# Second mixing of talking-heads attention: the last 64 keys of two neighbouring tiles in one matmul, with the values held in five blocks

## The chip, the cores and the metric

The kernel runs on one core of a Trainium2 chip. The metric is device time in microseconds (us). The kernel before takes 595.45 us as the median of three runs (595.12 to 597.32). The engines in the profile are PE (TensorE, matmuls), PEld (its weight loads), DVE (VectorE), ACT (ScalarE), POOL (GpSimd) and SP (which issues DMAs).

## The reference

Attention with two mixings over heads, followed by a feed-forward layer with squared ReLU. There are 8 batches, 12 heads, 448 positions and a head size of 64; the layer goes from 768 to 2048 to 768 features.

```python
scores = scale * np.matmul(q, k.transpose(0, 1, 3, 2))
scores = np.einsum('bhij,hg->bgij', scores, w_pre)       # first mixing
scores = scores - np.max(scores, axis=-1, keepdims=True)
attn = np.exp(scores)
attn = attn / (np.sum(attn, axis=-1, keepdims=True) + 1e-09)
attn = np.einsum('bhij,hg->bgij', attn, w_post)          # second mixing
out = np.matmul(attn, v)
h = np.maximum(x @ w_in, 0.0)      # x: out with the heads side by side
return h * h @ w_out
```

## The kernel before

The work goes in 360 steps, 45 for each batch. A step handles one tile of 10 queries (`IQ`; the last tile of a batch has 8) with all 12 heads, which is 120 rows (`RG`) of 448 keys.

Scores of 128 queries at a time are made by `score_burst` and copied out of PSUM by ACT and VectorE. DMAs on the SP queue (`gather`) then put the rows of one tile, query by query with its heads, into one buffer `G`. For the first 20 tiles of batch 0 (`FUSED`) there is no gather; the queries are multiplied by the mixing weights on VectorE instead (`mix_queries`).

`mix` (L391) is the first half of a step. One matmul with a 120x120 matrix mixes the heads (L402); ACT takes the exponential `e` and its row sums `sm` (L405); VectorE takes the reciprocals `rc` (L407); POOL multiplies the rows of the second mixing's matrix `post` by them, giving `pn` (L409). So the division by the row sum is done on the small matrix and not on `e`.

`unmix` (L413) is the second half, four steps later (`LAG`). Four matmuls (L422) take 128 keys of `e` each as the stationary side and `pn` as the moving side, 120 columns. They turn the tile around (keys on partitions) and mix the heads. 448 keys are three blocks of 128 and one of 64. The fourth matmul takes keys 320 to 447, so that its lower 64 partitions repeat keys of the third block. All four land in one PSUM bank, and VectorE casts the 480 columns to `at` (L424).

After 15 tiles, a third of a batch, two `av_unit`s (L212) multiply by the values, six heads each. Per head there are four matmuls of 150 columns, one for each block of keys (L220). Two heads run beside each other, one in each half of the array's columns and of PSUM's partitions. ACT copies the result to `xt`. The values lie in `vts`, four blocks; the fourth has real rows in its upper 64 partitions alone, and zeros in the lower ones, set once by a memset (L165). `load_v` brings the values by POOL-issued DMAs, some 29 steps or more ahead of a batch's first value product for batches 2 to 7.

`ffn1_unit` (L260, with the ReLU on ACT and the squaring on POOL or VectorE, L271) and `ffn2_unit` (L304) are the feed-forward layer.

The order of TensorE's and POOL's instructions is the order in which the program writes them (`manual_schedule`). Feed-forward work of the batch before is put between `mix` and `unmix` in portions (`fill`), by fixed weights for each unit. VectorE's, ACT's and SP's order is made by the language's planner, which takes the dependencies and an estimate of each instruction's time. All PSUM tiles share one pool of eight banks.

Of the kernel before, what the change touches and what calls it, by code (L numbers as in the profile page):

```python
# [8 lines left out]
BF16 = mybir.dt.bfloat16  # L9
F32 = mybir.dt.float32  # L10
ACT = mybir.ActivationFunctionType
ALU = mybir.AluOpType
PE, POOL = mybir.EngineType.PE, mybir.EngineType.Pool

B, H, S, D = 8, 12, 448, 64
# [4 lines left out]
R = 4  # L20
RQ = 7
PQ = S // RQ
HQ = H // 2
IQ = 10
NT = 45
RG = H * IQ
FUSED = 20
# [10 lines left out]
TT = 15  # L38
TQ = TT * IQ
# [14 lines left out]
def kernel(  # L54
# [11 lines left out]
    nc = tc.nc  # L66
    P = nc.NUM_PARTITIONS

    consts = ctx.enter_context(tc.tile_pool(name="consts", bufs=1))
    wts = ctx.enter_context(tc.tile_pool(name="wts", bufs=1))  # L70
    stage = ctx.enter_context(tc.tile_pool(name="stage", bufs=1))
    work = ctx.enter_context(tc.tile_pool(name="work", bufs=1))
    atp = ctx.enter_context(tc.tile_pool(name="atp", bufs=1))
# [3 lines left out]
    def bank(name, dtype=F32):  # L77
        return psp.tile([P, 512 if dtype == F32 else 1024], dtype, name=name, tag="ps")
# [21 lines left out]
    def wcol(w, name, eng):  # L100
# [7 lines left out]
                      in_=bass.AP(tensor=w_pre.tensor, offset=w_pre[0, 0:1].offset, ap=[[0, P], [1, H * H]]))  # L108
# [24 lines left out]
    for t in range(3 * P // IQ, NT):  # L133
        n0, n = max(0, 3 * P - IQ * t), min(IQ, S - IQ * t)
# [11 lines left out]
    post = consts.tile([P, H, IQ], BF16, name="post")  # L146
    nc.vector.tensor_tensor(out=post[0:RG, :, :], in0=istripe[0:RG, :].unsqueeze(1).to_broadcast([RG, H, IQ]),
                            in1=col_post[0:RG, :].unsqueeze(2).to_broadcast([RG, H, IQ]), op=ALU.mult)
    post = post[:, :, :].rearrange("p g i -> p (g i)")
# [7 lines left out]
    post_gi = consts.tile([P, H, IQ], BF16, name="post_gi")  # L157
    nc.vector.tensor_tensor(out=post_gi[0:RG, :, :], in0=stripe_gi[0:RG, :].unsqueeze(1).to_broadcast([RG, H, IQ]),
                            in1=col_gi[0:RG, :].unsqueeze(2).to_broadcast([RG, H, IQ]), op=ALU.mult)
    post_gi = post_gi[:, :, :].rearrange("p g i -> p (g i)")  # L160
    ND = LAG + 2
    ets = [consts.tile([P, S], BF16, name=f"e{x}") for x in range(ND)]
    vts = [stage.tile([P, H, R, D], BF16, name=f"v{x}") for x in range(2)]
    for t in vts:
        nc.vector.memset(t[0:PQ, :, R - 1, :], 0.0)  # L165

    attn = [atp.tile([P, R, H, TQ], BF16, name=f"at{x}") for x in range(2)]
    w1 = [wts.tile([P, NPAIR, DFF // 2], BF16, name=f"w1_{x}") for x in range(2)]
    w2 = [wts.tile([P, FT // 4, DMODEL], BF16, name=f"w2_{x}") for x in range(4)]

    qTs, kTs, xts, h2ts, ats = {}, {}, {}, {}, {}
# [40 lines left out]
    def av_unit(b, third, cp):  # L212

        at = ats[(b, third)]
        ps = bank("ot_ps")
        for y in range(3):
            for r in range(R):
                for hh in range(2):
                    g = 6 * cp + 2 * y + hh
                    nc.tensor.matmul(ps[64 * hh:64 * hh + 64, TQ * y:TQ * y + TQ], lhsT=vts[b % 2][:, g, r, :],  # L220
                                     rhs=at[:, r, g, :], start=(y == 0 and r == 0), stop=(r == R - 1),
                                     skip_group_check=True)
        if b not in xts:
            xts[b] = ffnp.tile([P, NPAIR, S], BF16, name="xt", tag="xt", bufs=2)
        n = min(TQ, S - TQ * third)
        nc.scalar.copy(out=xts[b][:, 3 * cp:3 * cp + 3, TQ * third:TQ * third + n],  # L226
                       in_=ps[:, 0:3 * TQ].rearrange("p (y t) -> p y t", t=TQ)[:, :, 0:n])

    def av_units(b, third):
        return [(800, lambda cp=cp: av_unit(b, third, cp)) for cp in range(2)]  # L230
# [96 lines left out]
    Sb, Gs, esb = {}, {}, {}  # L327
# [27 lines left out]
    def rows_of(t):  # L355
        return H * min(IQ, S - IQ * t)
# [23 lines left out]
    def fused_part(t, u):  # L380

        if t not in parts:
            parts[t] = [0, bank("m_ps")]
        if parts[t][0] > u:
            return
        parts[t][0] = u + 1
        for y in range(2):
            nc.tensor.matmul(parts[t][1][0:RG, 0:S], rhs=kTs[0][:, u + 3 * y, :], lhsT=mixed(u, y, t, t + 1),  # L388
                             start=(u + y == 0), stop=(u + 3 * y == NPAIR - 1))

    def mix(s):  # L391
        n = rows_of(s[1])
        b, t = s
        fused = b == 0 and t < FUSED
        if fused:
            for u in range(NPAIR // 2):
                fused_part(t, u)
            ps = parts[t][1]
        else:
            ps = bank("m_ps")  # L400
            m = pres[max(x for x in pres if x <= t)] if b else pre
            nc.tensor.matmul(ps[0:n, 0:S], lhsT=m[0:n, 0:n], rhs=Gs.pop(s)[0:n, :], start=True, stop=True)  # L402
        e = ets[(NT * s[0] + s[1]) % ND]
        sm = work.tile([P, 1], F32, name="sm", tag="sm", bufs=4)
        nc.scalar.activation(out=e[0:n, 0:S], in_=ps[0:n, 0:S], func=ACT.Exp, scale=SCALE, accum_out=sm[0:n, 0:1])  # L405
        rc = work.tile([P, 1], F32, name="rc", tag="rc", bufs=4)
        nc.vector.reciprocal(out=rc[0:n, :], in_=sm[0:n, :])  # L407
        pn = work.tile([P, RG], BF16, name="pn", tag="pn", bufs=LAG + 2)
        nc.gpsimd.tensor_scalar(out=pn[0:n, :], in0=(post_gi if fused else post)[0:n, :], scalar1=rc[0:n, 0:1], scalar2=1.0,  # L409
                                op0=ALU.mult, op1=ALU.mult)  # L410
        esb[s] = (e, pn)

    def unmix(s):  # L413
        b, t = s
        n = rows_of(t)
        third, tl = divmod(t, TT)
        if (b, third) not in ats:
            ats[(b, third)] = attn[(3 * b + third) % 2]
        e, pn = esb.pop(s)
        ps = bank("at_ps")  # L420
        for r in range(R):
            nc.tensor.matmul(ps[:, RG * r:RG * r + RG], lhsT=e[0:n, min(P * r, S - P):min(P * r, S - P) + P], rhs=pn[0:n, :],  # L422
                             start=True, stop=True)
        nc.vector.tensor_copy(out=ats[(b, third)][:, :, :, IQ * tl:IQ * tl + IQ],  # L424
                              in_=ps[:, 0:R * RG].rearrange("p (r g i) -> p r g i", r=R, i=IQ))

    filler = []
    owed = [0.0]
# [17 lines left out]
    with tc.manual_schedule(engines={PE, POOL}):  # L446
# [39 lines left out]
        for i in range(-1, end):  # L486
# [9 lines left out]
            if s0:  # L496
                b, t = s0
# [9 lines left out]
            if s0:  # L507
                mix(s0)
# [4 lines left out]
            if s1:  # L513
                unmix(s1)
                b1, t1 = s1
                if t1 % TT == TT - 1:
                    for u in av_units(b1, t1 // TT):
                        at_step(i + 3, u)
                if t1 == NT - 1:
                    at_step(i + 3 if b1 else FFN2_AT, (0, lambda b1=b1: filler.extend(ffn_units(b1))))  # L520
# [4 lines left out]
            for _ in range(2 if i >= GATHERS_AT else 0):  # L525
# [8 lines left out]
                if nxt < len(blocks) and t2 - FIRST[b2][blk2] in first:  # L534
                    x = first.index(t2 - FIRST[b2][blk2])
# [37 lines left out]
```

## Time and profile before

| | |
|---|---|
| median of three runs | 595.45 us |
| profiled execution | 597.58 us, span 595.5 us |
| TensorE busy, share of the span | 573.0 us, 96% |
| VectorE busy | 411.7 us, 69% |
| ScalarE busy | 381.5 us, 64% |
| GpSimd busy | 311.7 us, 52% |
| granted TensorE clock, mean | 0.997 |
| L422, second mixing | 1440 matmuls, 134.9 us busy |
| L424, cast of its result | 360, mean 650 ns |
| L220, value product | 1152 matmuls, 42.2 us busy |
| L407, reciprocal | 360, mean 159 ns |
| L409, `pn` | 360, mean 370 ns |

Matmuls overlap, so that the mean duration of one (216 ns at L422) is longer than its share of TensorE's time. What one is worth is read from the chain of waits, which gives the path its times. Busy shares are means over the span; the windows by stage show the first batches apart from the rest.

### The profile page before, as it was taken

How to read it: one execution, taken by the hardware profiler on the slowest of the kernel's cores; microseconds unless marked ns; L12 is line 12 of the kernel's file. 1: busy time of each engine (PE TensorE's matmuls, PEld its weight loads, DVE VectorE, ACT ScalarE, POOL GpSimd, SP SyncE). 2: the span in 40 equal slices, each digit the busy share in tenths (PEclk: the TensorE clock that was granted, in tenths of full speed). 3: DMA queues.
4: the chain of work that ended last, by engine and by line, in shares of the span. 5: the costliest groups of instructions: out<-in, count | busy, mean ns of one | idle time of the engine just before them, and what ended most of it. 6: DMA issues, size and time to landing. Idle time of an engine off the chain costs nothing.

```text
span 595.5 us, 18405 instructions
## 1 busy us (share of the span) xinstructions
PE 573.0 (96%) x6615; PEld 370.2 (62%) x6615; DVE 411.7 (69%) x1073; ACT 381.5 (64%) x1114; POOL 311.7 (52%) x692
## 2 busy tenths in 40 slices
PE   3998999999999999999999999999999999999997
PEld 2576777666566665666665665666665665666554
DVE  7657669888767777767877678777867767666011
ACT  3645888677876557865776548775777648762410
POOL 6344885343677227762577326772386325761740
PEclk9998999999999999999999999999999999999999
DMA  9898899689568754696557855786544855432113
GB/s 130 136 181 156 144 206 184 141 141 196 118 117 135 160 117 89 113 149 140 107 96 129 157 119 100 117 136 141 121 74 65 138 120 105 86 49 54 28 26 81
DMA packets 79307, 71.49 MB, mean 120 GB/s; under 512 B 12496, under 2 KB 74224, under 8 KB 79216
## 3 DMA queue, kind: packets, MB, share of 16 engines
q1 hardware_dynamic: 49354, 47.30, 36.6%
q0 software_dynamic: 29280, 22.81, 28.3%
q8 instruction: 52, 0.85, 0.6%
q10 hardware_dynamic: 582, 0.21, 0.2%
q14 instruction: 39, 0.32, 0.1%
HBM read 45.70 MB, written 11.01 MB: 95 GB/s over the span
## 4 chain that ended last, share of the span: by engine, by line
PE 86%; DMA 4%; ACT 4%; issue 2%; POOL 1%; DVE 1%; SPq 0%; ACTq 0%; DVEq 0%; POOLq 0%
PE o_ps L304 24%; PE h_ps L260 24%; PE at_ps L422 12%; PE m_ps L402 10%; PE ot_ps L220 6%; PE m_ps L388 4%; PE s_ps L341 4%; DMA G<-S 3%; ACT e L405 2%; PE tr_ps L205 2%; ACT S L351 1%; DMA kst<-in_k_dram 1%; PE s_ps L347 1%; ACT hr L266 1%; POOL qst L87 1%
## 5 line engine op out<-in xcount | busy, mean ns | idle before, releaser
L424 DVE CAST at<-at_ps 128x480 bf16<-128x480 f32 x360 | 228.5, 650 | 67.4 <-PE at_ps L422 66.7
L405 ACT ACTIVATE e<-m_ps 120x448 bf16<-120x448 f32 x360 | 196.1, 550 | 90.2 <-PE m_ps L402 77.8
L409 POOL TENSOR_SCALAR pn<-post,rc 120x120 bf16<-120x120 bf16 (+1 forms) x340 | 125.3, 370 | 212.8 <-DVE rc L407 123.5
L260 PE MATMUL h_ps<-xt,w 128*128 128x448 bf16 (+2 forms) x960 | 169.7, 316 | 1.2 <-ACT e L405 0.7
L304 PE MATMUL o_ps<-w,h 128*128 128x384 bf16 x768 | 138.7, 326 | 0.0
L422 PE MATMUL at_ps<-pn,e 120*128 120x120 bf16 (+1 forms) x1440 | 134.9, 216 | 1.1 <-ACT S L351 1.0
L422 PEld LDWEIGHTS <-e 120*128 120x128 bf16 (+1 forms) x1440 | 104.7, 98 | 44.0 <-ACT S L351 2.2
L402 PE MATMUL m_ps<-G,pre 120*120 120x448 bf16 (+1 forms) x340 | 121.9, 358 | 1.6 <-ACT S L351 0.7
L260 PEld LDWEIGHTS <-w 128*128 128x128 bf16 x960 | 85.2, 98 | 58.0 <-issue 6.9
L271 POOL TENSOR_TENSOR h<-hr 128x384 bf16<-128x384 f32 (+1 forms) x144 | 106.1, 739 | 22.2 <-ACT hr L266 19.0
L266 ACT ACTIVATE hr<-h_ps 128x448 f32<-128x448 f32 (+2 forms) x160 | 75.5, 478 | 49.5 <-PE h_ps L260 32.8
L304 PEld LDWEIGHTS <-h 128*128 128x128 bf16 x768 | 73.0, 98 | 45.5 <-issue 2.5
L407 DVE RECIPROCAL rc<-sm 120x1 f32<-120x1 f32 x360 | 57.1, 159 | 49.5 <-ACT e L405 41.0
L351 ACT CAST S<-s_ps 128x448 bf16<-128x448 f32 x177 | 82.3, 548 | 13.2 <-PE s_ps L341 10.8
L353 DVE CAST S<-s_ps 128x448 bf16<-128x448 f32 x141 | 79.5, 615 | 2.7 <-DMA G<-S 1.4
L405 ACT ACTIVATION_READ_ACCUMULATOR e<-m_ps 120x1 f32 x360 | 75.2, 209 | 0.0
L313 DVE COPY osb<-o_ps 128x384 f32<-128x384 f32 x54 | 30.0, 556 | 49.4 <-PE o_ps L304 49.0
L402 PEld LDWEIGHTS <-pre 120*120 120x120 bf16 (+1 forms) x340 | 45.0, 132 | 21.7 <-issue 12.7
L220 PE MATMUL ot_ps<-at,v 128*64 128x150 bf16 x1152 | 42.2, 229 | 0.1
L226 ACT CAST xt<-ot_ps 128x450 bf16<-128x450 f32 (+1 forms) x48 | 25.5, 533 | 26.3 <-PE ot_ps L220 25.7
L341 PE MATMUL s_ps<-kT,qT 64*128 64x448 bf16 x276 | 40.9, 360 | 0.9 <-ACT e L405 0.5
L220 PEld LDWEIGHTS <-v 128*64 128x64 bf16 x1152 | 38.0, 109 | 4.0 <-issue 3.4
(51 smaller groups left out, 281.5 us busy)
## 6 DMA issues: line engine op xcount, KB each, us to landing
G<-S SPq DMA_DIRECT2D x276, 105.0 KB
out_dram<-osb SPq DMA_DIRECT2D x54, 192.0 KB
kst<-in_k_dram POOLq DMA_DIRECT2D x14, 336.0 KB, 6.6
qst<-in_q_dram POOLq DMA_DIRECT2D x14, 336.0 KB, 6.7
G<-S SPq DMA_DIRECT2D x70, 52.5 KB
v<-in_v_dram POOLq DMA_DIRECT2D x8, 384.0 KB, 9.7
w<-in_moe_w_in_dram POOLq DMA_DIRECT2D x6, 512.0 KB, 9.6
w<-in_moe_w_out_dram POOLq DMA_DIRECT2D x8, 384.0 KB, 8.1
```

What stands on the lines that cost most here:

```text
L220: nc.tensor.matmul(ps[64 * hh:64 * hh + 64, TQ * y:TQ * y + TQ], lhsT=vts[b % 2][:, g, r, :], rhs=at[:, r, g, :], start=(y == 0 and r == 0 ...
L260: nc.tensor.matmul(ps[:, 0:n], lhsT=w1[ft // 8][:, c2, ft % 8 * 128:ft % 8 * 128 + 128], rhs=xts[b][:, c2, n0:n1], start=(c2 == 0), stop=( ...
L266: nc.scalar.activation(out=hr[:, 0:n], in_=ps[:, 0:n], func=ACT.Relu)
L271: eng.tensor_tensor(out=dst[:, x - o:y - o], in0=hr[:, x - n0:y - n0], in1=hr[:, x - n0:y - n0], op=ALU.mult)
L304: nc.tensor.matmul(ps[:, 0:384], lhsT=lhsT, rhs=w2[ft // 4][:, ft % 4, nt * 384:(nt + 1) * 384], start=(ft == 0), stop=(ft == FT - 1))
L351: nc.scalar.copy(out=sb[:, h, :], in_=ps[:, 0:S])
L353: nc.vector.tensor_copy(out=sb[:, h, :], in_=ps[:, 0:S])
L402: nc.tensor.matmul(ps[0:n, 0:S], lhsT=m[0:n, 0:n], rhs=Gs.pop(s)[0:n, :], start=True, stop=True)
L405: nc.scalar.activation(out=e[0:n, 0:S], in_=ps[0:n, 0:S], func=ACT.Exp, scale=SCALE, accum_out=sm[0:n, 0:1])
L409: nc.gpsimd.tensor_scalar(out=pn[0:n, :], in0=(post_gi if fused else post)[0:n, :], scalar1=rc[0:n, 0:1], scalar2=1.0, op0=ALU.mult, op1=A ...
L422: nc.tensor.matmul(ps[:, RG * r:RG * r + RG], lhsT=e[0:n, min(P * r, S - P):min(P * r, S - P) + P], rhs=pn[0:n, :], start=True, stop=True)
L424: nc.vector.tensor_copy(out=ats[(b, third)][:, :, :, IQ * tl:IQ * tl + IQ], in_=ps[:, 0:R * RG].rearrange("p (r g i) -> p r g i", r=R, i=IQ))
```

## The change

In each third, tile 0 stands alone and the tiles 1 and 2, 3 and 4, up to 13 and 14 are pairs. `mix` now also divides the last 64 keys' exponentials of its tile by the row sum and writes them into one half of a buffer `en` that the two tiles of a pair share: lower half for an even tile, upper half for an odd one. This runs on VectorE, for the first 30 tiles of batch 0 on POOL. `unmix` keeps its first three matmuls. The fourth is done for even tiles alone: `en`, both halves, is the stationary side, and the undivided matrix `post` the moving one. It gives the last 64 keys of the even tile on the lower partitions and those of the odd tile before it on the upper ones. For odd tiles the cast takes 360 columns instead of 480.

In the value product the first three blocks stay as they were. The fourth becomes two matmuls, one for the eight even tiles (80 columns) and one for the seven odd ones (70 columns, which lie in the places of the even tiles behind them). Both go over every second group of ten columns. The even ones need the last 64 keys' values on the lower partitions: a fifth block of `vts`, whose lower half is a copy of the fourth block's upper half, made on VectorE once a batch, and whose upper half is zero.

```diff
     ets = [consts.tile([P, S], BF16, name=f"e{x}") for x in range(ND)]
-    vts = [stage.tile([P, H, R, D], BF16, name=f"v{x}") for x in range(2)]
+    ens = [consts.tile([P, 2, PQ], BF16, name=f"en{x}") for x in range(ND)]
+    for t in ens:
+        nc.vector.memset(t[:, :, :], 0.0)
+    vts = [stage.tile([P, H, R + 1, D], BF16, name=f"v{x}") for x in range(2)]
     for t in vts:
         nc.vector.memset(t[0:PQ, :, R - 1, :], 0.0)
-
-    attn = [atp.tile([P, R, H, TQ], BF16, name=f"at{x}") for x in range(2)]
+        nc.vector.memset(t[PQ:P, :, R, :], 0.0)
+
+    attn = [atp.tile([P, R, H, TT, IQ], BF16, name=f"at{x}") for x in range(2)]
...
     def av_unit(b, third, cp):
         at = ats[(b, third)]
+        if cp == 0 and third == 0:
+            nc.vector.tensor_copy(out=vts[b % 2][0:PQ, :, R, :], in_=vts[b % 2][PQ:P, :, R - 1, :])
         ps = bank("ot_ps")
         for y in range(3):
-            for r in range(R):
+            for r in range(R - 1):
                 for hh in range(2):
                     g = 6 * cp + 2 * y + hh
                     nc.tensor.matmul(ps[64 * hh:64 * hh + 64, TQ * y:TQ * y + TQ], lhsT=vts[b % 2][:, g, r, :],
-                                     rhs=at[:, r, g, :], start=(y == 0 and r == 0), stop=(r == R - 1),
+                                     rhs=at[:, r, g, :, :].rearrange("p t i -> p (t i)"),
+                                     start=(y == 0 and r == 0), stop=False, skip_group_check=True)
+            for x in range(2):
+                for hh in range(2):
+                    g = 6 * cp + 2 * y + hh
+                    cols = ps[64 * hh:64 * hh + 64, TQ * y:TQ * y + TQ].rearrange("p (t i) -> p t i", i=IQ)
+                    nc.tensor.matmul(cols[:, x:TT:2, :], lhsT=vts[b % 2][:, g, R - x, :],
+                                     rhs=at[:, R - 1, g, 2 * x:TT:2, :], start=False, stop=True,
                                      skip_group_check=True)
...
-        esb[s] = (e, pn)
+        en = ens[(8 * (3 * b + t // TT) + (t % TT + 1) // 2) % ND]
+        eng = nc.gpsimd if b == 0 and t < 2 * TT else nc.vector
+        eng.tensor_scalar(out=en[0:n, t % TT % 2, :], in0=e[0:n, S - PQ:S], scalar1=rc[0:n, 0:1], scalar2=1.0,
+                          op0=ALU.mult, op1=ALU.mult)
+        esb[s] = (e, pn, en)
...
-        e, pn = esb.pop(s)
+        e, pn, en = esb.pop(s)
         ps = bank("at_ps")
-        for r in range(R):
-            nc.tensor.matmul(ps[:, RG * r:RG * r + RG], lhsT=e[0:n, min(P * r, S - P):min(P * r, S - P) + P], rhs=pn[0:n, :],
+        for r in range(R - 1):
+            nc.tensor.matmul(ps[:, RG * r:RG * r + RG], lhsT=e[0:n, P * r:P * r + P], rhs=pn[0:n, :], start=True, stop=True)
+        k = R - 1 if tl % 2 else R
+        if k == R:
+            mat = post_gi if b == 0 and t < FUSED else post
+            nc.tensor.matmul(ps[:, RG * (R - 1):RG * R], lhsT=en[0:RG, :, :].rearrange("p x k -> p (x k)"), rhs=mat[0:RG, :],
                              start=True, stop=True)
-        nc.vector.tensor_copy(out=ats[(b, third)][:, :, :, IQ * tl:IQ * tl + IQ],
-                              in_=ps[:, 0:R * RG].rearrange("p (r g i) -> p r g i", r=R, i=IQ))
+        nc.vector.tensor_copy(out=ats[(b, third)][:, 0:k, :, tl, :],
+                              in_=ps[:, 0:k * RG].rearrange("p (r g i) -> p r g i", r=k, i=IQ))
```

## The prediction

> **What bounds the kernel now.** I read the page's busy shares and the clock row first, then who waited for whom, then the chain of waits, because the chain says what one instruction of each kind is worth on the path.
>
> ```profile
> PE 573.0 (96%) x6615; PEld 370.2 (62%) x6615; DVE 411.7 (69%) x1073; ACT 381.5 (64%) x1114; POOL 311.7 (52%) x692
> ...
> PE 86%; DMA 4%; ACT 4%; issue 2%; POOL 1%; DVE 1%; SPq 0%; ACTq 0%; DVEq 0%; POOLq 0%
> ```
>
> TensorE is busy 96% of the span and is 86% of the chain that ended last. Stage by stage (time, then busy time of each engine):
>
> ```profile
> 0.00:20.00 20.00, 9.69 (x188) 5.57 (x188) 14.12 (x38) 7.42 (x15) 10.92 (x23) 1.00 0.92 134
> 20.00:90.00 70.00, 66.88 (x887) 49.90 (x887) 48.07 (x132) 50.59 (x166) 43.13 (x98) 0.98 0.93 166
> 90.00:150.00 60.00, 57.26 (x868) 40.09 (x868) 51.79 (x161) 45.00 (x145) 25.96 (x60) 1.00 0.88 164
> 150.00:550.00 400.00, 398.14 (x4406) 251.20 (x4405) 293.07 (x736) 268.04 (x772) 214.42 (x481) 1.00 0.62 113
> ```
>
> From 150 to 550 us TensorE is idle 1.9 us of 400: whatever leaves its queue there comes off the time. From 20 to 150 us it is idle 5.9 us, so part of a saving may turn into waiting. VectorE is the second engine: 73% busy from 150 to 550 us, but 86% from 90 to 150 us. The chain of waits, a stretch of it (start, length, instructions):
>
> ```profile
> 281.56 0.21 PE at_ps L422 x4
> 281.77 0.19 PE m_ps L402
> 281.96 1.30 PE o_ps L304 x8
> ...
> 283.67 0.86 PE tr_ps L205 x84
> 284.52 1.69 PE ot_ps L220 x48
> ```
>
> One matmul of the second mixing (120 columns) is 0.21/4 = 52.5 ns of path. A 384-column one is 1.30/8 = 162.5 ns, one of 448 is 190 ns; the difference, 27.5 ns for 64 columns, is 0.43 ns a column, and 120 x 0.43 = 52 shows that weight loads are hidden. The value product is two matmuls side by side in half the array: 1.69/24 = 70.4 ns a pair, 64.5 of it streaming 150 columns and 5.9 over.
>
> **Part by part.**
>
> Removed: the fourth matmul of seven tiles in each third of 15. 8 batches x 3 thirds x 7 = 168 matmuls x 52.5 ns = 8.8 us, all on TensorE. For steps of batches 2 to 7 (126 of them) that is 6.6 us in the stretch with no idle time; for the first two batches 2.2 us.
>
> Changed: the value product. Each of 48 units has 3 groups (y); in each, one pair of 150 columns becomes a pair of 80 and a pair of 70. At 0.43 ns a column plus 5.9 ns a pair these are 40.3 + 36.0 = 76.3 ns against 70.4: +5.9 ns x 144 = +0.85 us. No row shows the 128x64 form at these lengths. From below: the columns streamed are the same, so 0; a gain is excluded by that count. From above: if a short pair costs what the long one does, 144 x 70.4 = +10.1 us. I take +0.85: the transposes, nearest in length at 64 columns with a weight load each, go at 0.86/84 = 10.2 ns apiece, four abreast, so a pair's loads do not hold back 70 columns.
>
> Its operands are also no longer contiguous: the moving side and the output go in runs of 10 columns with every second run left out. No row of before has that. Half the streaming rate would add 150 x 0.43 = 64.5 ns x 144 = 9.3 us; below, nothing. I take nothing, as runs of ten are still served by whole neighbouring pairs; the other end is a rival.
>
> The Trainium skill, "PSUM — Partial Sum Buffer", Specifications, says that any non-contiguous access pattern there slows matmuls significantly; no run here shows it, and by it the sum would lose its gain (the second rival's time).
>
> VectorE, its cast of the mixed weights: 168 of 360 shrink from 480 to 360 columns. From the rows 128x448 at 615 ns and 128x480 at 650 ns: 1.09 ns a column, 131 ns x 168 = -22 us of VectorE, off the path.
>
> VectorE, the new normalizing of 64 keys: 330 instructions (the other 30 on POOL). Nearest rows:
>
> ```profile
> 5.53 0.17 DVE L127 COPY order<-ident 120x48 bf16<-120x48 bf16 x1
> 5.61 0.17 DVE L128 COPY order<-ident 120x72 bf16<-120x72 bf16 x1
> ```
>
> So 0.17 us each; it also needs the reciprocal just ahead of it on the same engine, which is 0.16 us and today is followed by independent work after about 0.08 us (18.96 to 19.04), so up to 0.08 + 0.05 us more of waiting. 330 x 0.30 = 99 us at most, 330 x 0.17 = 56 us at least; I take 0.25, 82 us. Net +60 us: 472 of 590, 80%. Behind it in VectorE's queue stand the casts out of the PSUM banks, and TensorE waits for these only when the eight banks run out. Before, VectorE itself waits for TensorE's at_ps 123 times, so it usually arrives first:
>
> ```profile
> DVE at L424 <- PE at_ps L422: 66.7, 123, 1.1
> DVE osb L313 <- PE o_ps L304: 49.0, 44, 22.1
> DVE rc L407 <- ACT e L405: 41.0, 121, 2.3
> ```
>
> That waiting is the cover. From 150 to 550 us VectorE goes from 293 to about 293 + 60 x 400/550 = 337 of 394, 86%: covered on the mean, late in bursts. In 90 to 150 us it is 51.8 plus 40 steps x 0.25 less 2.5 = 59 of 60: the cover is gone. I put 1 us of TensorE waiting there; bounds 0 and 4 us.
>
> The 30 on POOL (first 30 tiles, until about 61 us): 120x120 is 370 ns and 128x64 291 ns there, so 0.3 x 30 = 9 us while POOL has over half its time free; what waits behind is its pn and its DMA issues, shifted by 0.3 us, and pn is used four steps (some 6 us) later. Zero; at worst 1 us.
>
> The copy of the last value block, one a batch: the memset of the same bytes is 378 ns; 8 x 0.4 = 3 us of VectorE. TensorE needs it only when a batch's first value product starts. The planner takes ready VectorE work ahead of its place (mixing written behind the first steps runs at 13 to 16 us), and v lands 9 us or more ahead of that use (the last issue for batch 1 is at 87.2 us, its product at 107 us). Zero; the other end is a rival. Eight extra memsets at the start, about 8 x 0.2 us, fall in the 2.37 us in which VectorE waits for `wall`: zero, at worst 1.5 us. No DMA is added, and the SP queue is untouched.
>
> Sum: -6.6 - 1.1 (half of 2.2; the idle of the first stages takes the rest) + 0.85 + 1 = -5.9, say -6.0 us. The profiled execution took 597.58 us (span 595.5 and 2.1 around it), so 591.6 by it; the median of the runs shown is 595.45, 2.1 lower, so 589.4.
>
> **Rivals.**
>
> Port rival, slower. VectorE's new instruction and POOL may hold each other up. Rows of before show such a thing:
>
> ```profile
> 92.19 0.80 POOL L409 TENSOR_SCALAR pn<-post,rc 120x120 bf16<-120x120 bf16 x2
> 92.30 0.46 DVE L271 TENSOR_TENSOR tails<-hr 128x64 bf16<-128x64 f32 x1
> ...
> 94.81 0.64 POOL L409 TENSOR_SCALAR pn<-post,rc 120x120 bf16<-120x120 bf16 x1 [0.35 <-DVE rc L407]
> 94.84 0.24 DVE L271 TENSOR_TENSOR h<-hr 128x84 bf16<-128x84 f32 x1
> 95.00 0.22 DVE L271 TENSOR_TENSOR tails<-hr 128x64 bf16<-128x64 f32 x1
> ```
>
> A 0.22 us VectorE instruction that starts under a running pn takes 0.46; a pn of 0.37 that meets two of VectorE's takes 0.64. Both pn and the new instruction start on the same reciprocal. If pn goes first, each new one waits up to 0.37 us, or up to 0.83 us behind POOL's squaring. At 0.25 us more each VectorE gains another 82 us: 90 to 150 us then wants 69 of 60 (+9 us), and the later stages 337 + 60 = 397 of 394 (+3 us, and some 2 us of bursts): -6 + 14 = +8, 603. It decides once the mean wait passes some 0.2 us. Against it: pn starts 0.17 us after a reciprocal ends (94.50 + 0.15 to 94.81), in which time the new one can be under way. 0.13.
>
> The Trainium skill, "SBUF — State Buffer", Who interferes with whom, says that a VectorE tensor_scalar in a two-port mode and a GpSimd instruction exclude each other, the second waiting for all of the first; the rows at 92 and 94 us agree (0.46 and 0.64 us), and by it this rival is real and only its size is open.
>
> Strided rival: short matmuls at half rate, +9.3 us: 595.45 - 6 + 9.3 = 598.7. For it speaks the new pattern alone; against it, that each run of ten stays whole. 0.08.
>
> Copy rival: the planner sets the copy where v has not landed (5.7 to 12.4 us from issue to landing). VectorE then stops, and TensorE some 4 us later (estimate: eight banks, about three taken in a step of 530/360 = 1.47 us): up to 4 us x 7 batches, 617; or it stands just ahead of the product behind late casts, some 1 us x 8, 597. 0.10.
>
> No-effect rival: TensorE's saving comes back as waits for ACT or the gather, or VectorE's bursts cost 4 to 6 us instead of 1: 593 to 597. For it: 4% of the chain is DMA; against it: 1.9 us of idle in 400. 0.15.
>
> **How the numbers follow.** Forecast 589.4 with 0.54, its own range 586.4 (all of 8.8 us lands) to 592.4 (bursts cost 4). 0.5%, 3 us, is about what a measurement can tell from no change. Faster: 0.54 + 0.03 of the no-effect case = 0.57. Same: 0.12 + 0.03 of the strided + 0.02 of the copy case = 0.17. Slower: 0.13 + 0.05 + 0.08 = 0.26. The range that leaves out no more than 2 in 10 goes from 586 to 603, the port rival's price.
>
> **What would show it.** at_ps matmuls 1272 instead of 1440, at 0.16 us of chain for three; ot_ps 1440 instead of 1152, a unit pair at 1.73 us instead of 1.69 (2.1 or more: the value product was underpriced). The new instruction at 0.17 us on VectorE; a mean over 0.35 speaks for the port rival, with pn over 0.4. VectorE near 80% busy, TensorE's waits for VectorE still under 2 us. I am wrong if TensorE's share falls below 95% or waits for `at` or the copied v appear.

## The result, and the profile after

The changed kernel takes 642.61 us (median of six runs) against 596.03 us before: a ratio of 1.078, 95% interval 1.074 to 1.083. The forecast was 589.4 us, in a range from 586 to 603.

The busy shares and the chain of the changed kernel:

```profile
span 641.7 us, 19027 instructions
...
PE 584.9 (91%) x6735; PEld 371.2 (58%) x6735; DVE 473.8 (74%) x1419; ACT 383.2 (60%) x1114; POOL 317.7 (50%) x722
...
PE 69%; DMA 13%; DVE 10%; ACT 3%; issue 3%; POOL 1%; DVEq 0%; POOLq 0%; ACTq 0%; SPq 0%
PE h_ps L273 21%; PE o_ps L317 19%; DMA v<-in_v_dram 10%; PE m_ps L415 8%; PE at_ps L439 7%; PE m_ps L401 4%; PE ot_ps L226 3%; PE s_ps L354 3%; DVE at L445 3%; ACT e L418 2%; DVE en L426 2%; PE tr_ps L209 2%; DVE S L366 1%; DMA G<-S 1%; PE at_ps L443 1%
```

TensorE is down from 86% of the chain to 69%. What came in is one transfer: 10% of the chain is the load of the values, of which the chain before showed nothing. The list of waits of the changed kernel (total, times, longest) names who waits for it:

```profile
DVE v L220 <- DMA v<-in_v_dram: 41.6, 7, 10.5
```

The longest of TensorE's own waits in the same kernel:

```profile
PE s_ps L354 <- DVE osb L326: 12.3, 3, 4.7
PE m_ps L415 <- DVE at L445: 11.1, 4, 10.5
PE s_ps L354 <- DVE at L445: 8.9, 5, 4.4
```

L220 is the copy of the last value block on VectorE, once a batch. In seven of eight batches VectorE stands still until v has landed, 10.5 us for batch 1 and (41.6 - 10.5)/6 = 5.2 us on the mean for the others. Before, TensorE waited for VectorE once:

```profile
PE m_ps L402 <- DVE at L424: 0.2, 1, 0.2
```

Now it waits for it 38.9 us in all. One of these places in order of time:

```profile
281.15 0.78 POOL L247 DMA_DIRECT2D v<-in_v_dram  x1
...
283.69 0.24 DVE L426 TENSOR_SCALAR en<-e,rc 120x64 bf16<-120x64 bf16 x1
...
285.72 0.55 PE L354 MATMUL s_ps<-kT,qT 64*128 64x448 bf16 x4
...
289.86 0.36 DVE L220 COPY v<-v 64x768 bf16<-64x768 bf16 x1 [5.92 <-DMA v<-in_v_dram]
290.13 0.52 DVE L445 CAST at<-at_ps 128x360 bf16<-128x360 f32 x1
...
290.70 0.56 PE L354 MATMUL s_ps<-kT,qT 64*128 64x448 bf16 x2 [4.43 <-DVE at L445]
```

The second half of v is issued at 281.15 us. VectorE reaches the copy at 283.93 us (283.69 + 0.24), 2.8 us after that issue, and waits to 289.86. These values are needed 20 us later, at 309.7 us, where the next batch's value product starts. Behind the copy stand the casts that free PSUM banks, and TensorE stops at 286.27 us (285.72 + 0.55).

The stop costs more than its length. The same place in windows (time, then busy time of PE, PEld, DVE, ACT, POOL, the granted clock, DMA share, GB/s):

```profile
284.00:286.00 2.00, 2.00 (x19) 1.20 (x18) 0.00 (x0) 1.12 (x4) 0.19 (x1) 1.00 1.10 158
286.00:291.00 5.00, 0.57 (x6) 0.12 (x2) 1.08 (x4) 0.97 (x2) 0.00 (x0) 0.75 0.47 112
291.00:295.00 4.00, 3.29 (x13) 1.59 (x12) 3.36 (x10) 1.17 (x3) 1.07 (x3) 0.50 0.40 102
295.00:300.00 5.00, 5.00 (x42) 3.05 (x41) 4.25 (x12) 2.79 (x8) 0.73 (x2) 0.97 0.42 56
```

For four microseconds after the stop TensorE is granted half its clock; eight matmuls of `o_ps` take 2.56 us of the chain there, and 1.30 once the clock is back:

```profile
292.51 2.56 PE o_ps L317 x8
...
295.82 1.30 PE o_ps L317 x8
```

The Trainium skill, "TensorE: Matmul & The Clock Gate", Part 1, says that an idle window of about 3.4 us puts the clock to half until it has been busy for as long; the 4.43 us stop and the 0.50 behind it agree. Shorter stops had it too, and there the measurement decides: of the seven stops of TensorE in this kernel (2.91 to 10.49 us, 33.7 us in all) the one of 2.91 us at 148.7 us is followed by a clock of 0.50 from 152.0 to 155.4 us, and in the kernel before one of 1.77 us at 52.8 us by 0.50 from 56 to 59 us. From which length on a stop lowers the clock is not settled by these traces.

### The profile page after: what moved, and what is told of

Same layout as the page of the kernel before. It is cut to its first block, busy times and chain, and to the rows that moved or that the text cites. A ratio compares the mean times of both kernels' runs of the same rounds, so it can differ in the third digit from the quotient of the medians.

```text
span 641.7 us, 19027 instructions
## 1 busy us (share of the span) xinstructions
PE 584.9 (91%) x6735; PEld 371.2 (58%) x6735; DVE 473.8 (74%) x1419; ACT 383.2 (60%) x1114; POOL 317.7 (50%) x722
## 4 chain that ended last, share of the span: by engine, by line
PE 69%; DMA 13%; DVE 10%; ACT 3%; issue 3%; POOL 1%; DVEq 0%; POOLq 0%; ACTq 0%; SPq 0%
PE h_ps L273 21%; PE o_ps L317 19%; DMA v<-in_v_dram 10%; PE m_ps L415 8%; PE at_ps L439 7%; PE m_ps L401 4%; PE ot_ps L226 3%; PE s_ps L354 3%; DVE at L445 3%; ACT e L418 2%; DVE en L426 2%; PE tr_ps L209 2%; DVE S L366 1%; DMA G<-S 1%; PE at_ps L443 1%
## 5 line engine op out<-in xcount | busy, mean ns | idle before, releaser
L422 POOL TENSOR_SCALAR pn<-post,rc 120x120 bf16<-120x120 bf16 (+1 forms) x340 | 123.4, 365 | 262.6 <-DVE rc L420 164.0
L445 DVE CAST at<-at_ps 128x480 bf16<-128x480 f32 (+1 forms) x360 | 208.1, 590 | 32.9 <-PE at_ps L443 22.9
L317 PE MATMUL o_ps<-w,h 128*128 128x384 bf16 x768 | 148.4, 341 | 0.0
L415 PE MATMUL m_ps<-G,pre 120*120 120x448 bf16 (+1 forms) x340 | 124.0, 365 | 17.1 <-DVE at L445 11.1
L439 PE MATMUL at_ps<-pn,e 120*128 120x120 bf16 x1080 | 117.2, 217 | 0.3 <-issue 0.2
L439 PEld LDWEIGHTS <-e 120*128 120x128 bf16 x1080 | 86.7, 99 | 47.0 <-issue 4.5
L317 PEld LDWEIGHTS <-h 128*128 128x128 bf16 x768 | 76.4, 102 | 53.3 <-issue 14.0
L426 DVE TENSOR_SCALAR en<-e,rc 120x64 bf16<-120x64 bf16 x330 | 101.4, 309 | 7.5 <-DVE rc L420 0.2
L366 DVE CAST S<-s_ps 128x448 bf16<-128x448 f32 x141 | 81.6, 613 | 1.4 <-DMA G<-S 0.8
L354 PE MATMUL s_ps<-kT,qT 64*128 64x448 bf16 x276 | 43.6, 367 | 22.8 <-DVE osb L326 12.3
L226 PE MATMUL ot_ps<-at,v 128*64 128x150 bf16 x864 | 41.6, 229 | 0.0
```

Of the source, the lines that this page charges most:

```text
L317: nc.tensor.matmul(ps[:, 0:384], lhsT=lhsT, rhs=w2[ft // 4][:, ft % 4, nt * 384:(nt + 1) * 384], start=(ft == 0), stop=(ft == FT - 1))
L366: nc.vector.tensor_copy(out=sb[:, h, :], in_=ps[:, 0:S])
L426: eng.tensor_scalar(out=en[0:n, t % TT % 2, :], in0=e[0:n, S - PQ:S], scalar1=rc[0:n, 0:1], scalar2=1.0, op0=ALU.mult, op1=ALU.mult)
L439: nc.tensor.matmul(ps[:, RG * r:RG * r + RG], lhsT=e[0:n, P * r:P * r + P], rhs=pn[0:n, :], start=True, stop=True)
L445: nc.vector.tensor_copy(out=ats[(b, third)][:, 0:k, :, tl, :], in_=ps[:, 0:k * RG].rearrange("p (r g i) -> p r g i", r=k, i=IQ))
```

## Experiments

Each ratio is against the kernel before, run on the same chip.

**The copy on POOL.** The copy theory: the whole loss is VectorE waiting for v with everything else queued behind it. The port theory, its rival: VectorE's new instruction and POOL hold each other up, and this alone keeps the change from paying.

```diff
-        if cp == 0 and third == 0:
-            nc.vector.tensor_copy(out=vts[b % 2][0:PQ, :, R, :], in_=vts[b % 2][PQ:P, :, R - 1, :])
...
+    def copy_v(b):
+        nc.gpsimd.tensor_copy(out=vts[b % 2][0:PQ, :, R, :], in_=vts[b % 2][PQ:P, :, R - 1, :])
...
+        for y in range(B):
+            at_load(8 if y == 0 else 62 if y == 1 else NT * y + 4, copy_v, y)
```

> The copy of the last value block is taken from VectorE and given to POOL, at a step written by hand that lies 12 or more steps behind the load and 4 or more ahead of the use; all else as in the changed kernel. Copy theory (the loss is VectorE waiting for v with everything else queued behind it): no wait for v is left, and the time is that of the blind sum, 586 to 591 us, ratio 0.985 to 0.992. Port theory (the new VectorE instruction and POOL hold each other up, and that alone keeps the change from paying): 596 us or more, ratio 1.00 to 1.02.

Measured 593.9 us, ratio 0.9972 (0.9948 to 0.9995). Run again later with more rounds:

> The kernel with the copy on POOL once more, beside the one above and with more rounds, for a narrower interval: 0.995 to 0.999 if the first measurement holds.

0.9985 (0.9965 to 1.0005). So the 7.8% are gone with the wait for v, of which the trace shows none, and the time is slightly below the kernel before or the same. It is not the 1% below that the forecast had: 593.9 us lies between the two theories' numbers. The profile of the first of the two:

```profile
PE 567.5 (96%) x6735; PEld 364.0 (62%) x6735; DVE 470.1 (80%) x1411; ACT 381.9 (65%) x1114; POOL 325.9 (55%) x730
```

TensorE runs the same 6735 matmuls as in the changed kernel, in 567.5 us instead of 584.9, at a mean granted clock of 0.999 instead of 0.964. The difference of the two spans, 641.7 - 589.7 = 52.0 us, is thus 17.4 us of slower clock and 34.6 us of TensorE standing idle (56.8 against 22.2). This execution was the fastest of ten of its kernel, so that the spans lie some 3 us further apart than the medians.

**The copy alone**, in the kernel before, into a block that no one reads.

```diff
-    vts = [stage.tile([P, H, R, D], BF16, name=f"v{x}") for x in range(2)]
+    vts = [stage.tile([P, H, R + 1, D], BF16, name=f"v{x}") for x in range(2)]
...
         at = ats[(b, third)]
+        if cp == 0 and third == 0:
+            nc.vector.tensor_copy(out=vts[b % 2][0:PQ, :, R, :], in_=vts[b % 2][PQ:P, :, R - 1, :])
```

> The kernel before with nothing of the change but the copy on VectorE into a fifth block that no one reads. Copy theory: seven waits of about 6 us and a slow TensorE clock behind them, ratio 1.05 to 1.08. Port theory: ratio within 0.995 to 1.01.

Ratio 1.0756 (1.0717 to 1.0795): the copy brings a loss of this size by itself. Its waits:

```profile
DVE v L216 <- DMA v<-in_v_dram: 40.9, 7, 9.0
```

**No copy, a third transfer instead.**

```diff
-        if cp == 0 and third == 0:
-            nc.vector.tensor_copy(out=vts[b % 2][0:PQ, :, R, :], in_=vts[b % 2][PQ:P, :, R - 1, :])
...
+        if x == 1:
+            load_v4(b)
+
+    def load_v4(b):
+        nc.gpsimd.dma_start(out=vts[b % 2][0:PQ, :, R, :],
+                            in_=v[b, :, :, :].rearrange("h (p r) d -> p h (r d)", r=RQ)[:, :, (RQ - 1) * D:RQ * D])
```

> No copy at all: a third transfer puts the same values into the fifth block, issued by POOL behind the two of load_v. Copy theory: as the first run, 586 to 592 us, some 0.7 us of POOL more a batch. Port theory: 596 us or more.

595.9 us, ratio 1.0004 (0.9978 to 1.0030): the loss is gone here too. This time also lies between the two theories' numbers.

**The copy on VectorE, but tied to a later place.** It takes a factor of 1.0 that is worked out from the cast of tile 11.

```diff
-        if cp == 0 and third == 0:
-            nc.vector.tensor_copy(out=vts[b % 2][0:PQ, :, R, :], in_=vts[b % 2][PQ:P, :, R - 1, :])
...
+        if t == 11:
+            one = work.tile([P, 1], F32, name="one", tag="one", bufs=2)
+            nc.vector.tensor_scalar(out=one[PQ:P, :], in0=ats[(b, third)][PQ:P, 0, 0, tl, 0:1], scalar1=0.0, scalar2=1.0,
+                                    op0=ALU.mult, op1=ALU.add)
+            nc.vector.tensor_scalar(out=vts[b % 2][0:PQ, :, R, :], in0=vts[b % 2][PQ:P, :, R - 1, :],
+                                    scalar1=one[PQ:P, 0:1], scalar2=1.0, op0=ALU.mult, op1=ALU.mult)
```

> The copy is on VectorE as in the changed kernel, but made to depend on the cast of tile 11 of its batch (its factor, one, is worked out from that cast's result), so that it can't be set ahead of it. If it is the place and not the engine that costs 46 us: no wait of VectorE for v, time as with the copy on POOL, 591 to 596 us, ratio 0.99 to 1.00. If VectorE itself is too full for the copy, or it holds POOL up: over 600 us.

595.0 us, ratio 0.9984 (0.9952 to 1.0016), and no wait for v in the trace. VectorE is not too full for the copy; it was set at the wrong place in VectorE's queue. This settles the cause of the 46 us.

**What keeps the rest of the forecast away?** First without the new instruction, on top of the copy on POOL, so that TensorE's saving stands nearly alone:

```diff
-        en = ens[(8 * (3 * b + t // TT) + (t % TT + 1) // 2) % ND]
-        eng = nc.gpsimd if b == 0 and t < 2 * TT else nc.vector
-        eng.tensor_scalar(out=en[0:n, t % TT % 2, :], in0=e[0:n, S - PQ:S], scalar1=rc[0:n, 0:1], scalar2=1.0,
-                          op0=ALU.mult, op1=ALU.mult)
+        en = None
...
-            nc.tensor.matmul(ps[:, RG * (R - 1):RG * R], lhsT=en[0:RG, :, :].rearrange("p x k -> p (x k)"), rhs=mat[0:RG, :],
+            nc.tensor.matmul(ps[:, RG * (R - 1):RG * R], lhsT=e[0:n, S - P:S], rhs=pn[0:n, :],
```

> As the first run (copy on POOL), but without the new instruction: the fourth matmul of an even tile takes its own exponentials and pn as before the change, so the last 64 keys of the odd tiles are left out of the result and those of the even ones stand in the wrong half; instruction counts on TensorE stay those of the changed kernel. Copy theory: at most 2 us faster than the first run, since VectorE's extra work is covered. Port theory: 6 us or more faster than the first run.

Ratio 0.9933 (0.9909 to 0.9957), 4.0 us below before. Against the copy on POOL (0.9972 and 0.9985) that is 2.3 to 3.1 us (its interval overlaps the first and lies just below the second): the new instruction costs a little, less than the 6 us of the port theory and, at these middles, somewhat more than the 2 us of the copy theory. The chains fit: VectorE has 7% of the chain with the copy on POOL (5% in the repeat), 1% without the new instruction, and 1% before the change. But even without it only 4.0 of the 7.7 us that TensorE was relieved of (8.8 less 1.1 for the value product) came off the time.

All divisions to POOL (copy on POOL, and `eng = nc.gpsimd`):

> Copy on POOL, and all 360 divisions of the last 64 keys on POOL, none on VectorE. VectorE falls from 470 to about 371 us busy, POOL rises from 326 to about 426. If VectorE's load and its meetings with POOL take the rest of the gain: 1.5 to 2.5 us faster than with the copy on POOL alone, some 591 to 592 us. If the rest is lost elsewhere: no faster than that kernel (593 to 595), or slower, as pn comes later in POOL's queue.

Ratio 1.0048 (1.0029 to 1.0067), slower. POOL rises to 418 us. VectorE falls to 395 us and not to 371: the instruction's records (98.9 us) overlap those of its neighbours, and VectorE is busy 394 us in the run without it as well. ACT now waits for POOL's pn, which it did for 1 us with the copy alone on POOL:

```profile
ACT e L419 <- POOL pn L423: 27.7, 28, 1.1
```

So VectorE's load can't be handed to POOL whole. Nor does a part help:

```diff
-        eng = nc.gpsimd if b == 0 and t < 2 * TT else nc.vector
+        eng = nc.gpsimd if (b == 0 and t < 2 * TT) or (b > 1 and (t < 9 or t >= 32)) else nc.vector
```

> Copy on POOL; the division of the last 64 keys goes to POOL for the tiles 0 to 8 and 32 to 44 of the batches 2 to 7, where POOL is free for over half its time, and stays on VectorE for the rest. If VectorE's load in the busy stretches is what takes 2 us of the gain: 1 to 2 us faster than the copy on POOL alone, ratio 0.994 to 0.996. If not: the same as that kernel, 0.996 to 0.999.

0.9978 (0.9955 to 1.0002), beside 0.9985 of the kernel without the split in the same comparison: no difference.

Score bursts later, since the score copies wait for gathers in these traces:

```diff
-    STARTS[_b], FIRST[_b], BURSTS[_b] = (0, 128, 256, 384), (0, 13, 26, 39), ([5, 8], [5, 8], [6], [0, 3])
+    STARTS[_b], FIRST[_b], BURSTS[_b] = (0, 128, 256, 384), (0, 13, 26, 39), ([6, 9], [6, 9], [7], [1, 4])
```

> Copy on POOL, and each burst of scores for the next block starts one tile later, so that the gathers out of the buffer that it overwrites have more time. If the missing 3 to 4 us are waits of the score copies for gathers: those waits (4.2 us in the trace with the copy on POOL) fall below 1 us and the time to 590 to 592. If not: within 1 us of that kernel, or slower, if the first gathers of a block now come late.

Ratio 1.0064 (1.0032 to 1.0096), slower; the waits for gathers went from 4.2 to 2.8 us only, and TensorE waits for casts up to 2.7 us at a time came in. So the run did not take the waits away, and decides nothing about them.

**What is a microsecond of TensorE worth here?** The kernel before with 168 matmuls more, and the run without the new instruction with 176 fewer (each diff is against the kernel named):

```diff
+        if tl % 2:
+            r = R - 1
+            nc.tensor.matmul(ps[:, RG * r:RG * r + RG], lhsT=e[0:n, S - P:S], rhs=pn[0:n, :], start=True, stop=True)
```

> The kernel before with the fourth matmul of each odd tile done twice, 168 matmuls more: 8.8 us of TensorE's queue added, nothing else. Full worth: ratio 1.014 to 1.016. Half: 1.006 to 1.009.

```diff
-        k = R - 1 if tl % 2 else R
+        k = R if tl % 2 == 0 and b == 0 and third < 2 else R - 1
```

> The run without the new instruction, and now without the fourth matmul of the even tiles as well from the third third of batch 0 on: 22 thirds x 8 = 176 matmuls fewer, and those casts 360 columns wide; the last 64 keys are left out of the result (old contents stand in their place). If TensorE's time is worth its full length, 176 x 52.5 ns = 9.2 us faster than that run, ratio 0.976 to 0.980. If waits behind it take half, as the missing part of the forecast suggests: 0.984 to 0.988.

The first gives 1.0113 (1.0069 to 1.0157): 6.7 us for 8.8 put in. The second gives 0.9796 (0.9758 to 0.9834): 8.2 us below the 0.9933 of the run that it starts from, for 9.2 taken out; it also makes 176 casts on VectorE smaller. The middles are three quarters to nine tenths of the length. The intervals are wide: the first holds half the length (4.4 us) as well as all of it, the second excludes half. The first relief, 4.0 of 7.7 us with an interval of 1.4 us to either side, is low beside them, but one common share of some 0.65 would fit all three.

One candidate for the missing time shows in the traces, a wait of the score copies for the gathers. The lines of the kernel before, then the copy on POOL, then without the new instruction:

```profile
DVE S L353 <- DMA G<-S: 1.4, 3, 0.9
...
ACT S L351 <- DMA G<-S: 1.2, 1, 1.2
```

```profile
ACT S L365 <- DMA G<-S: 2.1, 1, 2.1
DVE S L367 <- DMA G<-S: 2.1, 3, 1.7
```

```profile
DVE S L367 <- DMA G<-S: 3.9, 4, 2.7
...
ACT S L365 <- DMA G<-S: 3.8, 2, 3.0
```

The next scores are to be copied into a buffer that is still being gathered from: 2.6, 4.2 and 7.7 us in one profiled execution each. One such place, copy on POOL:

```profile
384.14 1.40 ACT L365 CAST S<-s_ps 128x448 bf16<-128x448 f32 x3 [2.13 <-DMA G<-S]
...
384.73 1.29 PE L274 MATMUL h_ps<-xt,w 128*128 128x448 bf16 x6 [2.17 <-ACT S L365]
```

And one without the new instruction, with the window behind it, where the granted clock (the last number but two) is 0.50:

```profile
133.79 1.40 ACT L365 CAST S<-s_ps 128x448 bf16<-128x448 f32 x3 [2.98 <-DMA G<-S]
...
134.38 0.48 PE L437 MATMUL at_ps<-pn,e 120*128 120x120 bf16 x3 [2.85 <-ACT S L365]
```

```profile
134.00:140.00 6.00, 5.62 (x26) 2.83 (x26) 3.89 (x10) 3.83 (x12) 0.96 (x3) 0.50 0.89 207
```

So without the new instruction a part of the missing 3.7 us is clock: its seven executions have a mean granted clock of 0.994, those of the kernel before beside them 0.997, and 0.003 of 592 us is some 2 us (an estimate). For the copy on POOL this is no answer: its clock is 0.998, and the kernel with the split divisions waits 0.9 us for gathers in its trace where the repeat beside it waits 4.6, in the same time (0.9978 and 0.9985). Nor does the wait need a TensorE that is ahead: the kernel with 168 matmuls more waits 6.9 us. A third score buffer, which would take this wait away, was not run. Where the rest of the 2 to 4 us goes is not shown.

## Why the prediction was wrong, step by step

The step that failed is the copy of the last value block, which I put at zero. I had both facts on the page: the planner takes ready VectorE work ahead of its place, and v lands 9 us or more ahead of its use. I read them as cover. They are the opposite: the planner took the copy ahead of its place by some 26 us in the place shown, to 2.8 us behind the issue of a transfer that landed 8.7 us after it. Over the seven batches VectorE reached the copy 2.6 to 7.1 us behind the issue, and waited 2.7 to 10.5 us. That the planner takes the transfer for landed by then is inferred from this; its estimate is on no record. Time to the use protects only an instruction that stays near its use. Both signs of being wrong that I had named came: TensorE's share is 91%, and VectorE waits for v.

The copy rival named this mechanism, with 0.10, and its price was too small in three terms. I allowed up to 4 us a batch, 28 in all; VectorE stood for 41.6 and TensorE stood idle 34.6 us longer. I let TensorE run on for 4 us after VectorE stops; in the place shown it ran for 2.3 (283.93 to 286.27 us). And I left out the clock, 17.4 us of slower matmuls by the comparison with the copy on POOL.

Without that wait the forecast of 589.4 us would still have been missed. The copy on POOL took 593.9 and 594.3 us, inside the 593 to 597 of the no-effect rival, which I gave 0.15: 0.9 to 1.7 us came off by the ratios, not 6.0.

The other steps, by the runs without the wait:

- The removed matmuls: 1080 + 192 = 1272 remain, three of them 0.16 us of the chain, as forecast. I counted 7.7 of 8.8 us as gain; the two runs that add and remove such matmuls give 0.76 and 0.89 of their length, so the pricing holds in kind, but the first relief brought 4.0 us, which stays open in part as said.
- The value product: from the starts in the trace, two units take 1.738 us up to the next instruction on the mean, before 1.692. Times 24 this is 1.1 us; forecast 0.85. The strided rival falls: short pairs in runs of ten columns go at nearly full rate.
- The Trainium skill, "PSUM — Partial Sum Buffer", Specifications, has any non-contiguous pattern slow matmuls significantly; here, with runs of ten fp32 words and every second run left out, the measurement says otherwise (1.1 us in all, where half rate would be 9.3).
- The smaller cast: 649 to 522 ns for 360 columns, 127 ns less; forecast 131.
- The new instruction: 302 ns on the mean, where the nearest rows had 170 and the sum took 250 with the wait in it. VectorE's net rise is 470.1 - 411.7 = 58 us, forecast 60. The 1 us of TensorE waiting set against it is 2.3 to 3.1 by the runs with and without it, inside its bounds of 0 and 4. The cover was read too well: VectorE waited for `at_ps` at 123 of 360 casts, which is a third and not "usually".
- The 30 on POOL: 0.32 us each, forecast 0.3.
- The port rival: the mechanism is there, its size is small. In the group of the copy on POOL, and at one place:

```profile
L427 DVE TENSOR_SCALAR en<-e,rc 120x64 bf16<-120x64 bf16 x330 | 98.9, 302 | 7.9 <-DVE rc L421 0.7
```

```profile
377.65 0.37 POOL L423 TENSOR_SCALAR pn<-post,rc 120x120 bf16<-120x120 bf16 x1
377.90 0.97 DVE L427 TENSOR_SCALAR en<-e,rc 120x64 bf16<-120x64 bf16 x1
377.99 0.83 POOL L285 TENSOR_TENSOR h<-hr 128x384 bf16<-128x384 f32 x1
```

The instruction starts under a running pn, and then lasts until POOL's squaring has ended too: 0.97 us. Its median is 0.241. Over all 330 the mean lies 0.302 - 0.241 = 0.06 us above that, below the 0.2 from which the rival was to decide. The Trainium skill, "SBUF — State Buffer", Who interferes with whom, says that the second of two such instructions waits for all of the first; this place agrees, and shows that it may wait for the next one as well. The rows at 92 and 94 us that the prediction set beside this rule show such blocking for squarings (`TENSOR_TENSOR`, two inputs), not for a tensor_scalar.

## What to carry to other kernels

Where a planner orders an engine, a small instruction that depends on a DMA alone is a hazard: it may be set close behind the transfer's issue, and everything behind it on that engine waits for the landing (here 2.7 to 10.5 us). Ask of each such instruction not when its result is needed but what stands behind it in its queue; tie it to a late result, write its place by hand, or give it to an engine whose order is written. A stall of TensorE can be paid a second time in clock: here seven stalls of 33.7 us in all brought 17.4 us of slower matmuls.

## What was not expected of the hardware

An idle stretch of TensorE of 4.43 us was followed by some 4 us at a granted clock of 0.50, one of 1.77 us in the kernel before by 3 us of it, and over seven stalls the same 6735 matmuls took 17.4 us longer. A VectorE instruction with a median of 0.24 us took up to 2.4 us beside a busy POOL. Matmuls of 70 and 80 columns in the half-array form, with operands in runs of ten, cost 1.1 us more in 48 units where I had kept 9 to 10 us open.
